# Attention units of the paired blocks: q and k loaded eight tokens to a partition, scores as two 32-row products, and the second weights' preparation on a new timetable

## The chip, the cores and the metric

One core of one Trainium2 chip. The metric is the device time of one execution in microseconds (us). The kernel before takes 1783.91 us, the median of 3 runs (1781.94 to 1783.98).

## The reference

Three layers in a row over 4608 tokens (8 sequences of 576) of 512 features. All inputs are float32.

```python
scores = scale * np.matmul(q_c, k_c.transpose(0, 1, 2, 4, 3))   # chunks of 64 tokens, 8 heads of 64
attn = np.exp(scores - np.max(scores, axis=-1, keepdims=True))
attn = attn / (np.sum(attn, axis=-1, keepdims=True) + 1e-09)
x = np.matmul(attn, v_c)                                        # back to 4608 x 512
xn = x / rms * rms_g
g = xn @ w_gate                                                 # 512 -> 1536
x = (g * (1.0 / (1.0 + np.exp(-g))) * (xn @ w_val)) @ w_out     # 1536 -> 512
h = x @ w_in                                                    # 512 -> 2048
out = (h * np.clip(h + 3.0, 0.0, 6.0) / 6.0) @ w_out2           # 2048 -> 512
```

## The kernel before, in words

The tokens go in nine blocks of 512. Each float32 operand of a large product is split into a high and a low half, and a product is three matmuls of 128x128 by 512 columns. The program has four stages, each a loop over TensorE's products: blocks 0 to 2 of the first layer one by one; blocks 3 to 8 of it in three **pairs** (two blocks at once, in a scheme of seven products for eight; `product`, L831, for the way up, `mm_down_a`, L845 to L848, for the way down); block 0 of the second layer; and its other blocks in four pairs.

Between the products a clock of **ticks** runs (`tick`, L980). `agenda` holds what is to be written into the program at each tick; entries of a tick are sorted by `turn`. During the first two pairs a tick is two products of six matmuls or one step of the way down, and a pair takes 66 ticks (`PAIR`). The first pair begins at tick `P0` = 72. So the order on every engine is fixed when the program is built, and each engine works its list strictly from the front.

**Attention** for the later blocks is done in units of 256 tokens (`Pair`): load q, k and v; turn q and k with VectorE's 32x32 transposes (`turn_q` L639, `turn_k` L643); scores on TensorE (L655), each a 64x64 product over the 64 features of a head; maximum, subtraction, exponential, sum, share; transpose of the result (L697); product with v (L715). Units 10 to 17 run under the first two pairs, four to a pair; `STEPS_P` says at which tick of a unit each step stands. In `parts_qk` q and k are loaded so that a partition holds 32 features of one token: runs of 128 bytes, 16 DMAs for q and 16 for k of a unit, 24 or 32 of each where a unit crosses the end of a sequence. `some(5)` in `tick` issues up to five of the queued parts at a tick, all from SP. SP also issues the operands of the pairs (`wo`, L409; `wd`, L415), 512 KB each, which `loads.ahead` asks for when a tile has been used up.

**Second weights.** `Stash` prepares the second layer's weights while the pairs run: eight slices, each with four raw loads issued by ScalarE (`sraw`, L234), steps on ScalarE, VectorE and GpSimd (`within`, `merge`, `part`, `half`), and stores back to DRAM, issued by ScalarE too (`keep_in`, L283; `keep_out`, L287). `Stash.plan` has the ticks of the steps from a slice's start; the starts were 6, 33, 58, 86, 112, 134, 153 and 172 ticks after `P0`.

All DMAs of SP and ScalarE take eight completion semaphores in turn, and an issue waits until the DMA that had its semaphore before has landed, whatever its data. `wo`, `wd`, raw weights and many others share one pool of 36 buffers (`wp`).

Of the kernel before, what the change touches and what calls it, by code (L numbers as in the profile page):

```python
# [10 lines left out]
F32 = mybir.dt.float32  # L11
# [3 lines left out]
ALU = mybir.AluOpType  # L15
AX = mybir.AxisListType


def _f32_of(word):
# [23 lines left out]
STEPS_P = (  # L43
    (0, ("turn_q",)),
    (1, ("turn_k",)),
    (3, ("scores", "top")),
    (4, ("less",)),
    (5, ("expo",)),
    (7, ("total", "share")),
    (10, ("trans_p", "out_p")),  # L50
    (12, ("values", "out_x", "square")),
    (13, ("squares",)),
)
STEPS = (
    (0, ("turn_q", "turn_k")),
# [10 lines left out]
def fused_kernel(  # L66
# [13 lines left out]
    nc = tc.nc  # L80
    B, H, S, D = q.shape
    NT, DM = out.shape
    CH = 64
    FA = w_gate.shape[1] // 128
    FB = w_in2.shape[1] // 128
# [4 lines left out]
    NP = H // 2  # L90
    scale = 1.0 / float(D) ** 0.5

    NQ = FB // 2
# [10 lines left out]
    sm_p = ctx.enter_context(tc.tile_pool(name="sm", bufs=4))  # L104
# [9 lines left out]
    PS = ps_p.tile([128, 8, 512], F32, name="PS")  # L114
    yd = [dr_p.tile([128, KD, N], F32, name=f"yd{b}") for b in range(NB)]
    ATT, GB, VB, YB = 0, 2, 3, 4
# [105 lines left out]
    def at(t, fn, *args, turn=2):  # L222
        agenda[t].append((turn, lambda: fn(*args)))
# [43 lines left out]
    class Stash:  # L267
# [40 lines left out]
        def plan(self, t0):  # L308
            self.h = {}
            r, w = self.r, self.w  # L310
            for d, fn, *args in (
                (0, r[0].load), (1, r[1].load), (3, r[0].within), (4, r[0].merge), (5, r[0].part),
                (6, self.keep_in, 0), (6, r[1].within), (7, r[1].merge), (8, r[1].part),
                (10, self.keep_in, 1), (10, self.sums), (11, self.half, 0), (11, w[0].load),
                (13, self.keep_in, 2), (13, self.half, 1), (14, w[1].load),
                (15, self.keep_in, 3), (16, w[0].within), (17, w[0].merge), (18, w[0].part),
                (19, self.keep_out, 0), (19, w[1].within), (20, w[1].merge), (21, w[1].part),
                (23, self.keep_out, 1),
            ):
                at(t0 + d, fn, *args, turn=4)  # L320

        def fetch_out(self, z):
            w = wp.tile([128, 2, 512], F32R, tag="w", name="w")
# [22 lines left out]
    stash = [Stash(i) for i in range(NQ)]  # L346
# [76 lines left out]
    def runs(t0, n):  # L423
        done = 0
        while done < n:
            b, s = divmod(t0 + done, S)
            step = min(n - done, S - s)
            yield done, step, b, s
            done += step

    class Att:
# [54 lines left out]
        def top(self):  # L486
            self.mx = sm_p.tile([128, 2, NP], F32, tag="mx", name="mx")
            nc.vector.tensor_reduce(out=self.mx, in_=self.s, axis=AX.X, op=ALU.max)
# [96 lines left out]
        def run(self, *steps):  # L585
            for st in steps:
                getattr(self, st)()
# [4 lines left out]
    class Pair:  # L592
# [13 lines left out]
        def parts_qk(self):  # L606

            self.q, self.k = self.buf("q"), self.buf("k")
            for dst, src in ((self.q, q), (self.k, k)):
                d = dst.rearrange("p (a u f) -> p a u f", a=NP, f=32)  # L610
                for off, n, b, s in runs(self.i * TP, TP):
                    u0, un = off // 32, n // 32
                    sv = src[b, :, s:s + n, :].rearrange("(a j) (u t) (g f) -> j g t a u f", j=2, t=32, f=32)
                    for j in range(2):
                        for g in range(2):
                            r = j * 64 + g * 32
                            if un < NP:
                                for u in range(un):
                                    nc.sync.dma_start(out=d[r:r + 32, :, u0 + u, :], in_=sv[j, g, :, :, u])
                                    yield  # L620
                            else:
                                for a in range(NP):
                                    nc.sync.dma_start(out=d[r:r + 32, a, u0:u0 + un, :], in_=sv[j, g, :, a])  # L623
                                    yield

        def parts_v(self):
            self.v = self.buf("v")
            d = self.v.rearrange("p (c a d) -> p c a d", a=NP, d=D)
            for off, n, b, s in runs(self.i * TP, TP):
                c = slice(off // CH, (off + n) // CH)  # L630
                for r in range(2):
                    for a in range(NP):
                        sv = v[b, 2 * a + (r ^ a & 1), s:s + n, :].rearrange("(c p) d -> p c d", p=CH)
                        nc.sync.dma_start(out=d[r * 64:(r + 1) * 64, c, a, :], in_=sv)
                        yield

        def turn_q(self):
            self.qT = self.buf("qT")
            nc.vector.transpose(out=self.qT, in_=self.q)  # L639

        def turn_k(self):
            self.kT = self.buf("kT")
            nc.vector.transpose(out=self.kT, in_=self.k)  # L643

        def scores(self):
            ps = PS[:, ATT:ATT + 2, :].rearrange("p j (t a k) -> p j t a k", t=2, a=NP)
# [95 lines left out]
                op=ALU.add,  # L742
            )

        def run(self, *steps):
            for st in steps:
                getattr(self, st)()

    XN = {}

# [120 lines left out]
    def split_act(t):  # L871
        hi = ah_p.tile([128, N], F32R, tag="ah", name="ah")
        lo = al_p.tile([128, N], F32R, tag="al", name="al")
        nc.scalar.copy(hi, t)  # L874
        nc.gpsimd.tensor_tensor(lo, t, hi.bitcast(F32), op=ALU.subtract)  # L875
        return hi, lo
# [32 lines left out]
    with tc.manual_schedule():  # L909
# [18 lines left out]
        sqs.pop(0)  # L928
        xf.pop(0)

        unit = [Pair(i) for i in range(NPR)]
        supply = deque()
        ready = set()

        def some(n):

            while n > 0 and supply:
                if next(supply[0][1], True):
                    ready.add(supply.popleft()[0])
                else:  # L940
                    n -= 1
# [38 lines left out]
        def tick():  # L980
            t = clock[0]
            for _, fn in sorted(agenda.pop(t, ()), key=lambda x: x[0]):
                fn()
            some(8 if t < 0 else 5)
            clock[0] += 1

        for blk, due in (
            (1, (-5, -4, -4, -4, -4, -4)), (2, (18, 19, 20, 21, 22, 23)), (3, (42, 43, 44, 45, 46, 47)),
            (4, (66, 67, 67, 67, 67, 67)),
            *((5 + n, tuple(P0 + n // 2 * PAIR + t for t in ((27, 29, 30, 31, 32, 33), (55, 57, 58, 58, 59, 60))[n % 2]))  # L990
              for n in range(4)),
        ):
            Rms(blk).plan(due)
        for i, t0 in (
            (2, -29), (3, -17), (4, -5), (5, 7), (6, 19), (7, 31), (8, 43), (9, 55),
            *((10 + 4 * p + n, P0 + p * PAIR + t) for p in range(2) for n, t in enumerate((0, 14, 29, 42))),
        ):
            plan_unit(i, t0)
        for n in range(2 * NI):
            Operands(*divmod(n, 2)).plan(5 * n + (n > 6) - 2 * (n == 6))  # L1000
        for f in range(FA):
            at(2 * f + 1, keep_w, f, turn=3)
        for i, t0 in enumerate((6, 33, 58, 86, 112, 134, 153, 172)):
            stash[i].plan(P0 + t0)

        S00, S01, S11, S3, S1, S2, S4 = range(7)
# [70 lines left out]
        fills = {p: x_ops(3 + 2 * p) for p in range(3)}  # L1077
        for p, t0 in ((0, 60), (1, P0 + PAIR - 14), (2, P0 + 2 * PAIR - 14)):
            for t in range(t0, t0 + 20):
                at(t, go, fills[p], 2 if p == 0 and t > 71 or p and t in (t0 + 9, t0 + 10) else 1)  # L1080
            for t in range(6):
                at((66 if p == 0 else P0 + p * PAIR - 8) + t, loads.ahead, 1)

# [46 lines left out]
        for p in range(3):  # L1130
# [91 lines left out]
            for n, (z, f) in enumerate(items):  # L1222
                if 0 < n < len(items) - 2:
                    nx.append(split_wp(gt(items[n + 2][1], items[n + 2][0])))
                mm_down_a(loads.t[p, "out", f, 0], nx[n], f == 0, f == FA - 1, yb[z])
                if f == FA - 1:
                    y_store(b + z, yb[z])
                if z == 0 and n < 6:
                    loads.ahead(1)
                if p == 2:  # L1230
                    if n == 12:
                        load_x2(0)
                        XS = [xn_p.tile([128, KD, N], F32R, tag=tag, name="xr") for tag in ("XH", "XL")]
                        xs[:] = [(XS[0][:, c, :], XS[1][:, c, :]) for c in range(KD)]
                    elif n == 18:
                        x2 = xf.pop(0)
                        x_split([x2[:, c, :] for c in range(KD)])
                        stream.ahead(6)
                    z = n - 2 if n < FB else n - 8
                    if n < FB and 0 <= z or n >= FB and FB - 2 <= z < FB:  # L1240
                        stash[z // 2].fetch_out(z % 2)
                tick()

        X = {}
# [52 lines left out]
        for f in range(FB):  # L1297
            bank = 6 + f % 2
            i, z = divmod(f, 2)
            low, top = ((0, 0), (2, 0)) if z == 0 else ((3, 0), (3, 1))  # L1300
            w2 = (stream.t[i, low[0]][:, low[1]], stream.t[i, top[0]][:, top[1]])
            mm_up(bank, lambda wi, c: w2[c // 2][:, wi, c % 2 * 128:(c % 2 + 1) * 128], xs)
            if z == 1:
                stream.ahead(3)
            s = sg_p.tile([128, N], F32, tag="sg", name="sg")
            relu(s, PS[:, bank, :])
            gate(s, PS[:, bank, :])
            a = split_act(s)
            if f > 0:
                go(fill, 2)  # L1310
            if prev is not None:
                mm_down_b(W["out2", f - 1], prev, f == 1, False, base=2)
            prev = a
# [96 lines left out]
```

## Time and profile before

| | |
|---|---|
| median of 3 runs | 1783.91 us |
| the profiled execution | 1777.24 us |
| its span, first to last instruction | 1775.5 us |
| TensorE busy (matmul) | 1687.8 us, 95% |
| VectorE, ScalarE, GpSimd busy | 55%, 41%, 31% |
| HBM | 180 GB/s over the span |

The profile's page has busy times by engine, 40 slices of the span, DMA queues, the chain of work that ended last, and groups of instructions. Other views of the same trace list one engine in order of time, who waited for whom, one source line with the minimum, median and maximum of its durations, and busy times of chosen stretches. PE is TensorE, PEld its weight loads, DVE VectorE, ACT ScalarE, POOL GpSimd, SP SyncE; a q behind a name (SPq, ACTq) is the engine's own sequencer, where DMAs are issued.

### The profile page before, as it was taken

What the parts mean: (1) busy time and instruction counts of PE and PEld (TensorE: products, weight loads), DVE (VectorE), ACT (ScalarE), POOL (GpSimd) and SP (SyncE); (2) the same over time, 40 slices, a digit from 0 to 9 for tenths busy, and PEclk for the clock granted to TensorE, in tenths of its full rate; (3) what the DMA queues carried; (4) which work ended last, traced back from release to release, by engine and by line L of the source; (5) the groups of instructions that cost most, each with busy time, mean ns of one, the idle gap of its engine ahead of it and who ended that gap; (6) DMA issues with size and microseconds to landing.
All of it is one profiled execution on the core that took longest, in us unless ns stands there. A gap on an engine that the chain in (4) does not pass through costs nothing.

```text
span 1775.5 us, 25261 instructions
## 1 busy us (share of the span) xinstructions
PE 1687.8 (95%) x9448; PEld 1376.1 (78%) x9448; DVE 985.3 (55%) x1372; ACT 724.0 (41%) x1119; POOL 551.9 (31%) x408
## 2 busy tenths in 40 slices
PE   4789999999898898899999999999999999999998
PEld 4567777887676676778888888888888888888887
DVE  7997655747454574567654433544554554465440
ACT  5454443544453444454544333333333333343332
POOL 2322434321224522255234622112411321141123
PEclk7799999999998999999999999999999999999999
DMA  9832776656786767885798864444144424423410
GB/s 261 238 71 35 215 229 184 171 146 191 212 266 197 212 204 210 269 279 188 268 323 288 336 230 166 173 142 162 60 157 140 142 97 141 142 95 142 143 67 29
DMA packets 321499, 320.49 MB, mean 181 GB/s; under 512 B 200416, under 2 KB 258784, under 8 KB 321248
## 3 DMA queue, kind: packets, MB, share of 16 engines
q1 hardware_dynamic: 264032, 248.60, 45.4%
q10 hardware_dynamic: 57344, 70.27, 11.4%
q8 instruction: 75, 1.23, 0.3%
q14 instruction: 48, 0.39, 0.1%
HBM read 246.42 MB, written 72.35 MB: 180 GB/s over the span
## 4 chain that ended last, share of the span: by engine, by line
PE 73%; DMA 9%; DVE 8%; SPq 4%; ACT 2%; issue 2%; POOL 1%; ACTq 0%; DVEq 0%; POOLq 0%
PE PS L831 30%; PE PS L820 8%; PE PS L853 7%; PE PS L854 7%; PE PS L857 7%; DMA wo<-ops 3%; PE PS L845 3%; PE PS L848 3%; PE PS L846 3%; SPq L623 2%; DVE w L194 1%; DMA v<-in_v_dram 1%; DMA wraw<-in_moe_w_out_dram 1%; PE PS L715 1%; DMA k<-in_k_dram 1%
## 5 line engine op out<-in xcount | busy, mean ns | idle before, releaser
L831 PE MATMUL PS<-xu,wo 128*128 128x512 f32 x1512 | 356.9, 395 | 20.0 <-DMA wo<-ops 13.9
L831 PEld LDWEIGHTS PS<-xu,wo 128*128 128x128 f32 x1512 | 284.0, 190 | 86.0 <-DMA wo<-ops 9.4
L831 PE MATMUL PS<-xo,wq 128*128 128x512 f32 x1344 | 309.2, 389 | 0.0
L875 POOL TENSOR_TENSOR al<-sg,ah 128x512 fp32r<-128x512 f32 x84 | 120.5, 1434 | 582.4 <-PE PS L857 294.2
L831 PEld LDWEIGHTS PS<-xo,wq 128*128 128x128 f32 x1344 | 252.2, 188 | 52.4
L853 PE MATMUL PS<-w,ah 128*128 128x512 f32 x576 | 224.2, 389 | 0.0
L854 PE MATMUL PS<-w,ah 128*128 128x512 f32 x576 | 224.1, 389 | 0.0
L820 PE MATMUL PS<-XH,w 128*128 128x512 f32 x576 | 150.5, 403 | 11.3 <-DVE sg L1104 5.5
L857 PE MATMUL PS<-w,al 128*128 128x512 f32 x576 | 154.3, 389 | 0.0
L820 PEld LDWEIGHTS PS<-XH,w 128*128 128x128 f32 x576 | 109.5, 193 | 39.6 <-DVE sg L1104 6.9
L853 PEld LDWEIGHTS PS<-w,ah 128*128 128x128 f32 x576 | 108.1, 188 | 22.7 <-ACT ah L874 0.3
L854 PEld LDWEIGHTS PS<-w,ah 128*128 128x128 f32 x576 | 108.2, 188 | 22.5
L857 PEld LDWEIGHTS PS<-w,al 128*128 128x128 f32 x576 | 108.1, 188 | 22.4
L845 PE MATMUL PS<-gs,wd 128*128 128x512 f32 x288 | 115.5, 401 | 9.2 <-ACT gs L1123 4.2
L846 PE MATMUL PS<-gs,wd 128*128 128x512 f32 x288 | 113.4, 394 | 0.0
L1333 DVE TENSOR_TENSOR u<-u,PS 128x512 f32<-128x512 f32 x32 | 22.0, 688 | 156.4 <-PE PS L831 147.3
L1124 POOL TENSOR_TENSOR gs<-gu,gs 128x512 fp32r<-128x512 f32 x60 | 84.3, 1420 | 46.8 <-ACT gs L1123 41.5
L874 ACT CAST ah<-sg 128x512 fp32r<-128x512 f32 x84 | 52.2, 621 | 98.6 <-DVE sg L1104 69.8
L1128 DVE TENSOR_TENSOR gu<-gu,PS 128x512 f32<-128x512 f32 x60 | 40.9, 683 | 72.7 <-PE PS L831 34.3
L242 DVE TENSOR_SCALAR sc<-sc 128x512 f32<-128x512 f32 x32 | 19.7, 616 | 108.6 <-ACT sc L241 89.1
L820 PE MATMUL PS<-XL,w 128*128 128x512 f32 x288 | 79.2, 397 | 0.0
L848 PE MATMUL PS<-gs,wd 128*128 128x512 f32 x288 | 78.5, 395 | 0.1
(198 smaller groups left out, 2693.6 us busy)
## 6 DMA issues: line engine op xcount, KB each, us to landing
wq<-stash_in SPq DMA_DIRECT2D x152, 512.0 KB, 3.9
wo<-ops SPq DMA_DIRECT2D x126, 512.0 KB, 5.7
wd<-keep_out SPq DMA_DIRECT2D x36, 512.0 KB, 5.2
ops<-w ACTq DMA_DIRECT2D x36, 256.0 KB, 3.5
yd<-yst SPq DMA_DIRECT2D x18, 512.0 KB, 4.0
sraw<-in_moe_w_in_dram ACTq DMA_DIRECT2D x16, 512.0 KB, 6.8
stash_in<-slo ACTq DMA_DIRECT2D x32, 256.0 KB, 4.5
sraw<-in_moe_w_out_dram ACTq DMA_DIRECT2D x16, 512.0 KB, 5.3
```

What stands on the lines that cost most here:

```text
L820: nc.tensor.matmul(ps, w(wi, c), xs[c][xi], start=(i == 0), stop=(i == n - 1))
L831: nc.tensor.matmul(PS[:, bank, :], op[:, wi, c * 128:(c + 1) * 128], x[xi][:, c, :], start=first and i == 0, stop=last and i == 5, skip_gr ...
L845: nc.tensor.matmul(ps, wm[0], a[0], start=first, stop=False)
L846: nc.tensor.matmul(ps, wm[1], a[0], start=False, stop=False)
L848: nc.tensor.matmul(PS[:, banks[m], :], w[:, 0, m * 128:(m + 1) * 128], a[1], start=False, stop=last)
L853: nc.tensor.matmul(PS[:, base + m, :], am, w[:, 0, :], start=first, stop=False)
L854: nc.tensor.matmul(PS[:, base + m, :], am, w[:, 1, :], start=False, stop=False)
L857: nc.tensor.matmul(PS[:, base + m, :], a[1][:, m * 128:(m + 1) * 128], w[:, 0, :], start=False, stop=last)
L874: nc.scalar.copy(hi, t)
L875: nc.gpsimd.tensor_tensor(lo, t, hi.bitcast(F32), op=ALU.subtract)
L1124: nc.gpsimd.tensor_tensor(w[:, 1, :], t, w[:, 0, :].bitcast(F32), op=ALU.subtract)
L1128: nc.vector.tensor_tensor(o, x, y, op=op)
```

## The change

Units 10 to 17 become `Wide`, a subclass of `Pair`. A partition now holds eight tokens of one head in a run of 2 KB; four DMAs load q and four k (eight and eight across a sequence's end). The transposes write with a step of eight elements, so that the tokens come out in order, and a head's 64 features come to lie in two pieces on the same 32 partitions. So each score is two products over 32 rows that add up in PSUM, and the scores go in two halves (`scores0`, `scores1`), two ticks apart, each with a maximum of its own. The steps of a unit stand up to one tick later. `some` issues three parts at a tick instead of five from 14 ticks before `P0` on. The slices of the second weights start every 24 ticks and their steps are further apart; stores are written first in their tick instead of last; the last slice ends with the first tick of block 0 of the second layer, where a tick has been added to each step, and its two stored tiles are fetched at step 4 there.

```diff
 STEPS_P = (
     (0, ("turn_q",)),
     (1, ("turn_k",)),
-    (3, ("scores", "top")),
-    (4, ("less",)),
-    (5, ("expo",)),
-    (7, ("total", "share")),
-    (10, ("trans_p", "out_p")),
-    (12, ("values", "out_x", "square")),
-    (13, ("squares",)),
+    (3, ("scores0", "top0")),
+    (5, ("scores1", "top1")),
+    (6, ("less",)),
+    (7, ("expo",)),
+    (9, ("total", "share")),
+    (11, ("trans_p", "out_p")),
+    (13, ("values", "out_x", "square")),
+    (14, ("squares",)),
 )
...
                 (0, r[0].load), (1, r[1].load), (3, r[0].within), (4, r[0].merge), (5, r[0].part),
-                (6, self.keep_in, 0), (6, r[1].within), (7, r[1].merge), (8, r[1].part),
-                (10, self.keep_in, 1), (10, self.sums), (11, self.half, 0), (11, w[0].load),
-                (13, self.keep_in, 2), (13, self.half, 1), (14, w[1].load),
-                (15, self.keep_in, 3), (16, w[0].within), (17, w[0].merge), (18, w[0].part),
-                (19, self.keep_out, 0), (19, w[1].within), (20, w[1].merge), (21, w[1].part),
-                (23, self.keep_out, 1),
+                (9, r[1].within), (10, r[1].merge), (11, r[1].part), (13, self.sums),
+                (14, self.half, 0), (14, w[0].load), (18, self.half, 1), (18, w[1].load),
+                (19, w[0].within), (20, w[0].merge), (21, w[0].part),
+                (25, w[1].within), (26, w[1].merge), (27, w[1].part),
             ):
                 at(t0 + d, fn, *args, turn=4)
+            for d, fn, n in (
+                (7, self.keep_in, 0), (13, self.keep_in, 1), (16, self.keep_in, 2), (20, self.keep_in, 3),
+                (23, self.keep_out, 0), (29, self.keep_out, 1),
+            ):
+                at(t0 + d, fn, n, turn=1)
...
+    class Wide(Pair):
+        def parts_qk(self):
+            self.q, self.k = self.buf("q"), self.buf("k")
+            for dst, src in ((self.q, q), (self.k, k)):
+                d = dst.rearrange("p (h x) -> p h x", h=2)
+                for off, n, b, s in runs(self.i * TP, TP):
+                    for g in range(4):
+                        h = g // 2 + 2 * (g % 2)
+                        sv = src[b, h:h + 5:4, s:s + n, :].rearrange("h (t u) d -> t h (u d)", u=8)
+                        r = g * 32 + off // 8
+                        nc.sync.dma_start(out=d[r:r + n // 8], in_=sv)
+                        yield
+        def turned(self, to, x):
+            nc.vector.transpose(
+                out=to.rearrange("p (h g t u) -> p h u g t", h=2, g=2, u=8),
+                in_=x.rearrange("p (h u g f) -> p h u g f", h=2, u=8, g=2),
+            )
+        def scores(self, e):
...
+            for t in range(2):
+                for h in range(2):
+                    for g in range(2):
+                        for c in range(2):
+                            for j in range(2):
+                                f = slice((2 * j + e) * 32, (2 * j + e + 1) * 32)
+                                n = slice((2 * t + c) * 64, (2 * t + c + 1) * 64)
+                                nc.tensor.matmul(
+                                    ps[c * 64:(c + 1) * 64, j, t, 2 * h + e, :],
+                                    qT[f, g, h, n],
+                                    kT[f, g, h, n],
+                                    start=g == 0,
+                                    stop=g == 1,
+                                )
...
-        unit = [Pair(i) for i in range(NPR)]
+        unit = [(Pair if i < 10 else Wide)(i) for i in range(NPR)]
...
-            some(8 if t < 0 else 5)
+            some(8 if t < 0 else 5 if t < P0 - 14 else 3)
...
-            *((10 + 4 * p + n, P0 + p * PAIR + t) for p in range(2) for n, t in enumerate((0, 14, 29, 42))),
+            *((10 + 4 * p + n, P0 + p * PAIR + t) for p in range(2) for n, t in enumerate((0, 14, 28, 42))),
...
-        for i, t0 in enumerate((6, 33, 58, 86, 112, 134, 153, 172)):
+        for i, t0 in enumerate(range(1, 1 + 24 * NQ, 24)):
             stash[i].plan(P0 + t0)
```

On **SP**, at the start of the first pair: the order before, from the last operand tile asked for ahead of it. `q<-in_q_dram` and `k<-in_k_dram` are parts of unit 11, `wo<-ops_133` and so on the pairs' operands; x5 is five in a row.

```order
L409 DMA wo<-ops_133 128x1024 x2
L619 DMA q<-in_q_dram 32x4x32 x5
L409 DMA wo<-ops_134 128x1024
L619 DMA q<-in_q_dram 32x4x32 x3
L623 DMA q<-in_q_dram 32x6x32 x2
L409 DMA wo<-ops_134 128x1024
L623 DMA q<-in_q_dram 32x6x32 x5
L409 DMA wo<-ops_134 128x1024
L623 DMA q<-in_q_dram 32x6x32 x5
L409 DMA wo<-ops_134 128x1024
```

The same place in the changed program:

```order
L413 DMA wo<-ops_133 128x1024 x2
L772 DMA q<-in_q_dram 8x2x512 x3
L413 DMA wo<-ops_134 128x1024
L772 DMA q<-in_q_dram 8x2x512
L772 DMA q<-in_q_dram 24x2x512 x2
L413 DMA wo<-ops_134 128x1024
L772 DMA q<-in_q_dram 24x2x512 x2
L772 DMA k<-in_k_dram 8x2x512
L413 DMA wo<-ops_134 128x1024
```

Between the same operand loads stand at most three parts instead of five; q of this unit is through after 8 parts instead of 24, and the whole list has 80 parts of q and k for units 11 to 17 instead of 288.

On **PE**, unit 10 in the first pair before (`kT,qT` are scores, `ident,p` the transposes of the result, `qT,v` the products with v, `xu,wo` the pair's products):

```order
L831 MATMUL PS<-xu,wo 128x512 x48
L655 MATMUL PS<-kT,qT 64x64 x32
L831 MATMUL PS<-xu,wo 128x512 x84
L697 MATMUL PS<-ident,p 128x128 x8
L831 MATMUL PS<-xu,wo 128x512 x24
L715 MATMUL PS<-qT,v 64x64 x32
```

and in the changed program:

```order
L891 MATMUL PS<-xu,wo 128x512 x48
L794 MATMUL PS<-kT,qT 64x64 x32
L891 MATMUL PS<-xu,wo 128x512 x24
L794 MATMUL PS<-kT,qT 64x64 x32
L891 MATMUL PS<-xu,wo 128x512 x72
L704 MATMUL PS<-ident,p 128x128 x8
L891 MATMUL PS<-xu,wo 128x512 x24
L722 MATMUL PS<-qT,v 64x64 x32
```

A unit now breaks into the large products four times instead of three, with 32 more small products.

## Rows read from the trace of the kernel before

**Rows 1.** Busy times by stretch: first, second, third pair; second layer. (us, then by engine)

```profile
412.60:637.50 224.90, 206.35 (x1341) 164.74 (x1341) 128.18 (x161) 102.20 (x156) 74.92 (x53) 0.96 0.74 217
637.50:849.40 211.90, 199.43 (x1341) 160.67 (x1340) 127.63 (x162) 103.72 (x158) 77.96 (x55) 0.99 0.74 230
849.40:1030.60 181.20, 180.19 (x793) 148.53 (x793) 87.21 (x117) 76.26 (x132) 79.61 (x58) 1.00 0.86 311
1030.60:1775.50 744.90, 740.18 (x3265) 612.35 (x3263) 347.68 (x484) 246.72 (x388) 190.85 (x144) 1.00 0.37 130
```

**Rows 2.** Chain that ended last, second layer: start, us, what.

```profile
1142.46 9.52 PE PS L831 x42
```

**Rows 3.** PE in order of time, unit 10: start, us, what.

```profile
423.62 1.16 PE L655 MATMUL PS<-kT,qT 64*64 64x64 f32 x64
424.72 19.34 PE L831 MATMUL PS<-xu,wo 128*128 128x512 f32 x84
443.90 1.03 PE L697 MATMUL PS<-ident,p 128*128 128x128 f32 x8
444.69 5.70 PE L831 MATMUL PS<-xu,wo 128*128 128x512 f32 x24
450.32 1.16 PE L715 MATMUL PS<-qT,v 64*64 64x64 f32 x64
451.41 0.97 PE L831 MATMUL PS<-xu,wo 128*128 128x512 f32 x3
```

**Rows 4.** PE's waits, first two pairs: us in total, times, longest us.

```profile
PE PS L831 <- DMA wo<-ops: 13.9, 8, 3.9
PE PS L845 <- ACT gs L1123: 4.2, 3, 2.2
PE PS L845 <- DVE gu L1128: 2.8, 2, 2.2
...
PE PS L655 <- DVE kT L643: 2.7, 1, 2.7
```

**Rows 5.** SP in order of time, first pair: start, us, what.

```profile
474.82 1.22 SPq L409 DMA_DIRECT2D wo<-ops  x2
476.09 6.44 SPq L623 DMA_DIRECT2D q<-in_q_dram  x10
482.57 0.99 SPq L409 DMA_DIRECT2D wo<-ops  x2
```

**Rows 6.** SP's waits, first two pairs: us in total, times, longest us.

```profile
SPq L623 <- DMA wo<-ops: 25.7, 23, 2.7
...
SPq L634 <- DMA wo<-ops: 8.8, 8, 2.4
SPq L409 <- DMA stash_in<-shi: 7.2, 1, 7.2
```

**Rows 7.** Lines L623 and L634: ns of one issue, minimum, median, maximum.

```profile
L623 SPq DMA_DIRECT2D q<-in_q_dram x128: 311/439/1224, 423.0 to 760.2; - x128
...
L634 SPq DMA_DIRECT2D v<-in_v_dram x80: 465/606/1232, 455.8 to 789.3; - x80
```

**Rows 8.** ACT's waits, first two pairs: us in total, times, longest us.

```profile
ACT gu L1199 <- DMA k<-in_k_dram: 8.6, 2, 6.3
ACT sc L241 <- DMA k<-in_k_dram: 8.3, 4, 4.1
```

**Rows 9.** DMA issues, first two pairs: count, KB each, us to landing.

```profile
stash_in<-slo ACTq DMA_DIRECT2D x20, 256.0 KB, 3.8
...
q<-in_q_dram SPq DMA_DIRECT2D x64, 32.0 KB, 3.6
```

**Rows 10.** Lines L655, L643 and L738: ns of one, minimum, median, maximum.

```profile
L655 PEld LDWEIGHTS PS<-kT,qT x1024: 129/135/223, 91.0 to 792.0; 64*64 64x64 f32 x171
...
L643 DVE STREAM_TRANSPOSE kT<-k x16: 1186/1203/1246, 89.1 to 784.9; 128x1024 f32<-128x1024 f32 x16
...
L738 DVE TENSOR_REDUCE sqs<-kT x16: 1958/1986/2054, 125.5 to 821.0; 128x256 f32<-128x1024 f32 x16
```

More of the change, by code (lines that the diff above doesn't have):

```diff
@@ L635, in parts_v @@
                         yield
+        def turned(self, to, x):
+            nc.vector.transpose(out=to, in_=x)
         def turn_q(self):
             self.qT = self.buf("qT")
-            nc.vector.transpose(out=self.qT, in_=self.q)
+            self.turned(self.qT, self.q)
         def turn_k(self):
             self.kT = self.buf("kT")
-            nc.vector.transpose(out=self.kT, in_=self.k)
+            self.turned(self.kT, self.k)
         def scores(self):
@@ L743, in squares, with run, turned, top @@
             )
-        def run(self, *steps):
-            for st in steps:
+        def run(self, st):
+            if st[-1].isdigit():
+                getattr(self, st[:-1])(int(st[-1]))
+            else:
                 getattr(self, st)()
+    class Wide(Pair):
[10 more added lines that the diff above has]
+                        yield
+        def turned(self, to, x):
+            nc.vector.transpose(
[3 more added lines that the diff above has]
+        def scores(self, e):
+            ps = PS[:, ATT:ATT + 2, :].rearrange("p j (t a k) -> p j t a k", t=2, a=NP)
+            self.s = PS[:, ATT:ATT + 2, :].rearrange("p j (x k) -> p j x k", k=CH)
+            qT, kT = (
+                x.rearrange("p (h g n) -> p g h n", h=2, g=2) for x in (self.qT, self.kT)
+            )
[12 more added lines that the diff above has]
+                                    stop=g == 1,
+                                )
+        def top(self, e):
+            if e == 0:
+                self.mx = sm_p.tile([128, 2, 2 * NP], F32, tag="mx", name="mx")
+            nc.vector.tensor_reduce(
+                out=self.mx[:, :, e::2], in_=self.s[:, :, e::2, :], axis=AX.X, op=ALU.max
+            )
@@ L989, in fused_kernel @@
             (4, (66, 67, 67, 67, 67, 67)),
-            *((5 + n, tuple(P0 + n // 2 * PAIR + t for t in ((27, 29, 30, 31, 32, 33), (55, 57, 58, 58, 59, 60))[n % 2]))
+            *((5 + n, tuple(P0 + n // 2 * PAIR + t for t in ((28, 30, 31, 32, 33, 34), (56, 58, 59, 59, 60, 61))[n % 2]))
               for n in range(4)),
@@ L1079, in fused_kernel @@
             for t in range(t0, t0 + 20):
-                at(t, go, fills[p], 2 if p == 0 and t > 71 or p and t in (t0 + 9, t0 + 10) else 1)
+                at(t, go, fills[p], 2 if p == 0 and t > 71 or p and t in (t0 + 10, t0 + 11) else 1)
             for t in range(6):
@@ L1238, in fused_kernel @@
                         stream.ahead(6)
-                    z = n - 2 if n < FB else n - 8
-                    if n < FB and 0 <= z or n >= FB and FB - 2 <= z < FB:
-                        stash[z // 2].fetch_out(z % 2)
+                    if 1 < n < FB:
+                        stash[(n - 2) // 2].fetch_out(n % 2)
                 tick()
@@ L1308, in fused_kernel @@
             a = split_act(s)
+            tick()
+            if f == 4:
+                for z in range(2):
+                    stash[NQ - 1].fetch_out(z)
             if f > 0:
```

## The prediction

> **What bounds the kernel now.** I first cut the span into stages. In the second layer TensorE is busy for 740.18 of 744.9 us at the full 2.4 GHz clock (granted 1.00), and nothing there can be gained except with fewer products [rows 1]. The chain that ended last gives the price of a product: 42 in 9.52 us, 0.2267 us each [rows 2]. A pair has 7 x 6 x 12 = 504 products on its way up and 24 x 12 = 288 on its way down, 792 in all, so 792 x 0.2267 = 179.5 us. The third pair, which has no attention in it, takes 181.2 us: it is at that price. The first takes 224.9 and the second 211.9 us [rows 1], so 45.4 and 32.4 us more than their products.
>
> Part of that is attention on TensorE. From the start of unit 10's scores (423.62) to the product after its last step (451.41) pass 27.79 us, in which 84 + 24 products stand: 24.48 us [rows 3]. So a unit costs 3.31 us, four of them 13.2, and the two sums for the root mean square of a pair about 0.9 us (four products). The first pair then loses 45.4 - 14.1 = 31.3 us and the second 18.3 us, **49.6 us together**, to something that the third does not have. This is all that the change can win back.
>
> What is it? PE's longest waits in the two pairs are for operand tiles, 13.9 us; then come waits for ScalarE's and VectorE's results, 4.2 and 2.8 us, and 2.7 us for a turned k [rows 4]. The granted clock is 0.96 and 0.99 there [rows 1]: after an idle stretch the array goes at 1.2 GHz for a while. A mean of 0.96 over 224.9 us is 8% of the time at half speed, some 9 us lost beside the idle time; 0.99 is some 2 us.
>
> Why are the tiles late? SP's order of time shows it: two operand tiles issued at 474.82, then ten parts of q, 6.44 us, and only then the next two tiles at 482.57 [rows 5]. So two tiles go out in 7.75 us, while TensorE uses one up in two products of six matmuls, 2.7 us. One issue of q takes 0.439 us in the middle (L623, 128 for q, as many for k, and 16 each at L619), one of v 0.606 us [rows 7]. In the two pairs 288 parts of q and k take 288 x 0.439 = 126 us of SP's 437 us. And the parts wait as well: for operand tiles that they have nothing to do with, 25.7 us in 23 waits, and v's parts 8.8 us [rows 6], because DMAs share eight semaphores. The same reaches ScalarE, whose own DMA issues wait for k's parts: its work at L1199 is held 8.6 us by k's loads and at L241 8.3 us [rows 8]. ScalarE's list stands still then, and with it the results that PE waits for. So several of PE's rows have one cause, **too many small DMAs**.
>
> **The change part by part.**
>
> *Loads.* 288 parts become 80. Their issue is not in the trace; the bounds are the shortest q issue, 0.311 us, and v's longest, 1.232 us [rows 7]: 25 to 99 us, against 126. I take 0.44, the nearest form (same queue, same three-dimensional source), so 35 us: SP gets some 91 us back, over 40 us in either pair. A part now carries 128 KB instead of 32; q's landed in 3.6 us, ScalarE's 256 KB stores in 3.8 [rows 9], so I expect under 4 us, and a semaphore is held no longer than now. With at most three parts to a tick instead of five, the operand tiles that TensorE needs go out every 2.7 us. Of the 49.6 us I take 40 as won back: the waits for tiles and k and for what ScalarE could not start, and the slow clock behind each. Bounds: 24, if about half only changes its name, and all 49.6.
>
> *Scores.* Eight units have a second half, with as many matmul instructions again, and one more break into the large products. One half is 1.10 us (423.62 to 424.72) [rows 3], and about 0.2 us go at the two edges, since 3.31 is 0.3 more than its three pieces: 1.3 us, x 8 = **10.4 us, on the path**, since TensorE has nothing to hide it under. The lower bound is nothing, if it falls into waits that remain. The upper bound is in rival 3.
>
> *Transposes, maxima.* The transposes now write every eighth element. One takes 1.20 us now; the sum over squares (L738) handles 1024 elements too, but reads them with a long step, and takes 1.99 us [rows 10]. So 16 transposes cost 0 to 0.8 us more each, 13 us at most. VectorE is busy 128.18 of 224.9 us [rows 1] and PE's waits for it are 2.8 us [rows 4], so I take nothing; if the cover is gone, rival 2. The Trainium skill (SBUF — State Buffer, section "Door 1: The DMA port swizzle") says that accesses which leave a 16-byte line at each element pay a penalty, and eight float32 are 32 bytes. By that rule the transposes are slower; L738's row agrees with it, and the sum would be up to 13 us worse. The maximum in two halves costs VectorE an instruction more per unit, under the same cover.
>
> *Second weights.* The same steps on the same engines, 24 ticks apart instead of 19 to 28, with more room between steps, so a store waits less for the engine that makes its data, and ScalarE behind it too. The first two pairs get slightly more of it, and the end of the last slice falls into block 0 of the second layer, which has no slack; one store and two fetched tiles there have ten steps of time. I take zero, from 2 us less to 4 more.
>
> **Sum.** -40 + 10.4 = -29.6 us, so -30. The profiled execution took 1777.24 us, of which 1775.5 are the span, and would become 1747; it lies 6.7 us under the median, which I take as the base: 1783.9 - 30 = **1754 us**.
>
> **Rivals.**
>
> 1. *New waits take over half.* ScalarE, VectorE and GpSimd carry slightly more of the second weights in the two pairs, and scores in halves move subtraction and exponential a tick or two closer to the next unit. For it: PE already waits 4.2 and 2.8 us for their results [rows 4]. Against: much of that is held by DMAs [rows 8]. Then 24.8 us come back: 1783.9 - 24.8 + 10.4 = 1769.5. Chance 0.15.
>
> 2. *The step of eight shows.* The transposes cost 13 us more and stand before evictions that PE waits for: 1767. Chance 0.05. That is the rule of the Trainium skill named above, on the path.
>
> 3. *Slower: the 32-row products lose their overlap.* Now a half is 16 rounds of four products on four parts of the array, 0.07 us to a round, and a weight load of 0.135 us hides under them [rows 3, 10]. If with 32 rows it did not hide, each of 16 halves would be 16 x 0.135 = 2.2 us longer: 35 us, and 1754 + 35 = 1789. It decides when a half costs 30 / 16 = 1.9 us more than now. Against it: loads hide now although two neighbours in the order use the same rows, and the new order alternates rows. Chance 0.05.
>
> 4. *The tiles stay late for another reason.* An operand tile's issue also waits for its buffer, 7.2 us once behind a store of the second weights [rows 6]. If only 10 us come back, the scores eat them: 1784. For: the tiles share one pool with the raw weights. Against: such waits are few, the ones behind parts many. Chance 0.05.
>
> **How the numbers follow.** My forecast has 0.70, with 1743 (all 49.6 back, scores 8.8, and a little from ScalarE) to 1764. The range should leave out 2 in 10 at most: 1743 to 1772 adds rivals 1 and 2 and leaves out 3 and 4 and the edges. A measurement tells about 0.2%, 3.6 us, from no change. Faster by more: forecast, rivals 1 and 2, 0.90; within it, mostly rival 4, 0.04; slower, mostly rival 3, 0.06.
>
> **What would show it.** First and second pair take 195 to 210 us each instead of 225 and 212, the third still 181. SP has 80 parts of q and k of about 0.44 us, PE's wait for operand tiles falls from 13.9 us to under 4, the granted clock in the first pair rises to 0.99 or more, ScalarE's waits for k's loads are gone. Each half of the scores takes about 1.1 us. Transposes of 2.0 us speak for rival 2, halves of 3 us for rival 3. I am wrong if the waits for tiles stay, or if their place is taken by waits for ScalarE and VectorE of over 20 us.

## The result, and the profile after

The changed kernel takes 1753.64 us (median of 4 runs, 1748.98 to 1754.57) beside 1783.54 us for the kernel before (median of 4 runs as well): a ratio of 0.9829, with a 95% interval of 0.9810 to 0.9848. The forecast was 1754.

The span of the profiled execution goes from 1775.5 to 1746.8 us. Busy times by stretch, cut at the same places as [rows 1] (us, then PE, PEld, DVE, ACT, POOL busy with their counts, granted clock, DMA share, GB/s):

```profile
411.70:615.30 203.60, 200.65 (x1598) 163.90 (x1597) 133.89 (x167) 101.17 (x156) 76.19 (x54) 1.00 0.79 243
615.30:819.80 204.50, 202.27 (x1597) 163.35 (x1596) 140.71 (x170) 105.89 (x162) 81.82 (x57) 1.00 0.75 247
819.80:1001.20 181.40, 179.78 (x793) 148.59 (x792) 86.54 (x111) 74.32 (x129) 76.92 (x55) 1.00 0.80 290
1001.20:1746.80 745.60, 740.38 (x3265) 612.56 (x3264) 348.09 (x484) 246.93 (x388) 191.08 (x144) 1.00 0.38 131
```

All of it lies in the first two pairs: 224.9 and 211.9 us became 203.6 and 204.5, 28.7 us in all. The third pair and the second layer stayed within 1 us. The clock is granted in full, where it was 0.96 and 0.99. VectorE is busy for 274.6 us there, the two pairs together, instead of 255.8.

Who PE waited for, in the two pairs (us in total, times, longest us), to be held against [rows 4]:

```profile
PE PS L891 <- DVE gu L1188: 2.2, 1, 2.2
PE PS L908 <- POOL gs L1184: 0.8, 1, 0.8
PE PS L794 <- DVE kT L776: 0.7, 2, 0.6
PE PS L905 <- ACT gs L1183: 0.5, 2, 0.3
```

The row of 13.9 us for operand tiles is gone altogether. These are all waits above 0.4 us.

SP in order of time at the beginning of the first pair (start, us, what):

```profile
428.30 0.35 SPq L413 DMA_DIRECT2D wo<-ops  x1
428.70 1.00 SPq L772 DMA_DIRECT2D k<-in_k_dram  x3
430.54 0.35 SPq L413 DMA_DIRECT2D wo<-ops  x1
431.31 3.10 SPq L772 DMA_DIRECT2D k<-in_k_dram  x4
434.57 7.62 SPq L413 DMA_DIRECT2D wo<-ops  x7
```

In [rows 5] it was ten parts of q between two pairs of tiles. After the seven tiles at 434.57 SP comes to the first part of v, for which it waits 11.7 us until TensorE has done its products with v (L722); the part goes out at 454.63. So SP is ahead and waits for TensorE instead of the other way round. Before and after, in the two pairs (us in total, times, longest us):

```profile
SPq L634 <- PE PS L715: 9.3, 4, 3.0
```

```profile
SPq L638 <- PE PS L722: 49.2, 7, 11.7
```

One issue of q or k now takes (L772; ns minimum, median, maximum):

```profile
L772 SPq DMA_DIRECT2D q<-in_q_dram x44: 273/380/1517, 360.4 to 714.5; - x44
L772 SPq DMA_DIRECT2D k<-in_k_dram x44: 273/316/1122, 363.8 to 720.3; - x44
```

Of the 88, eight belong to unit 10 and go out before the first pair. What has not gone away is the waiting of these parts for other DMAs: SP's waits still have

```profile
SPq L772 <- DMA wo<-ops: 29.6, 14, 4.6
```

against 25.7 us in [rows 6]. TensorE no longer waits for a tile behind them. ScalarE's waits for DMAs come to 22 us in the two pairs, where they came to 83. The largest row is 6.4 us, in two pieces:

```profile
ACT gs L1183 <- DMA v<-in_v_dram: 6.4, 2, 4.8
```

and the two rows for k's loads of [rows 8] have no successor.

The scores of unit 10 on PE (start, us, what), and the lines of the scores and of the transposes (ns minimum, median, maximum), beside [rows 3, 10]:

```profile
422.69 1.16 PE L794 MATMUL PS<-kT,qT 32*64 32x64 f32 x64
423.78 5.73 PE L891 MATMUL PS<-xu,wo 128*128 128x512 f32 x24
429.44 1.16 PE L794 MATMUL PS<-kT,qT 32*64 32x64 f32 x64
430.53 16.62 PE L891 MATMUL PS<-xu,wo 128*128 128x512 f32 x72
```

```profile
L794 PEld LDWEIGHTS PS<-kT,qT x1024: 127/133/133, 422.7 to 765.5; 32*64 32x64 f32 x171
...
L776 DVE STREAM_TRANSPOSE qT<-q x8: 2124/2168/2237, 412.7 to 751.9; 128x1024 f32<-128x1024 f32 x8
L776 DVE STREAM_TRANSPOSE kT<-k x8: 2106/2155/2196, 417.1 to 753.9; 128x1024 f32<-128x1024 f32 x8
```

From 423.78 to 430.53 are 6.75 us, of which 24 products take 5.44: a half of the scores costs 1.31 us, at unit 10. The transposes became 0.93 (q) and 0.95 us (k) longer each, and TensorE waited 0.7 us in all for them.

### The profile page after: what moved, and what is told of

It reads as the page before. It is cut to its first block, busy times and chain, and to the rows that moved or that the text cites. A ratio compares the mean times of both kernels' runs of the same rounds, so it can differ in the third digit from the quotient of the medians.

```text
span 1746.8 us, 26052 instructions
## 1 busy us (share of the span) xinstructions
PE 1688.1 (97%) x9960; PEld 1380.9 (79%) x9960; DVE 1002.8 (57%) x1380; ACT 723.2 (41%) x1119; POOL 555.1 (32%) x408
## 4 chain that ended last, share of the span: by engine, by line
PE 52%; DVE 1%; DMA 0%; ACT 0%; issue 0%; POOL 0%; SPq 0%; DVEq 0%; POOLq 0%
PE PS L891 24%; PE PS L913 7%; PE PS L917 7%; PE PS L914 7%; PE PS L880 2%; PE PS L908 1%; PE PS L905 1%; PE PS L906 1%; DMA x<-yd 0%; DVE xf L841 0%; DVE xt L1093 0%; DVE sraw L252 0%; DVE sg L1351 0%; DVE sc L243 0%; POOL al L935 0%
## 5 line engine op out<-in xcount | busy, mean ns | idle before, releaser
L891 PE MATMUL PS<-xu,wo 128*128 128x512 f32 x1512 | 351.9, 392 | 3.0 <-DVE gu L1188 2.2
L905 PE MATMUL PS<-gs,wd 128*128 128x512 f32 x288 | 113.6, 394 | 2.1 <-DVE gu L1188 1.6
L906 PE MATMUL PS<-gs,wd 128*128 128x512 f32 x288 | 112.2, 390 | 0.0
L908 PE MATMUL PS<-gs,wd 128*128 128x512 f32 x288 | 77.1, 390 | 0.8 <-POOL gs L1184 0.8
L950 DVE TENSOR_SCALAR ost<-PS 128x512 f32<-128x512 f32 x26 | 16.5, 685 | 102.1 <-PE PS L917 102.1
```

What stands on the lines that cost most here:

```text
L891: nc.tensor.matmul(PS[:, bank, :], op[:, wi, c * 128:(c + 1) * 128], x[xi][:, c, :], start=first and i == 0, stop=last and i == 5, skip_gr ...
L905: nc.tensor.matmul(ps, wm[0], a[0], start=first, stop=False)
L906: nc.tensor.matmul(ps, wm[1], a[0], start=False, stop=False)
L908: nc.tensor.matmul(PS[:, banks[m], :], w[:, 0, m * 128:(m + 1) * 128], a[1], start=False, stop=last)
```

## The experiments

The kernels ran in three series, each on one chip beside runs of the kernel before. Ratios are to the kernel before, with their 95% intervals. "The pairs" are the first two together, from the profiled execution: 436.8 us before, 408.1 in the changed kernel. A profiled execution is one of several and can lie some 5 to 8 us off the median (1783.92 us for the 224 parts below, with a median of 1778.37), so the pairs' times are no finer than that.

### The new loads and scores without the new timetable

The second weights' starts, steps and the place of the last fetches are those of the kernel before; all else is the change.

```diff
...
-        for i, t0 in enumerate(range(1, 1 + 24 * NQ, 24)):
+        for i, t0 in enumerate((6, 33, 58, 86, 112, 134, 153, 172)):
             stash[i].plan(P0 + t0)
```

> The changed kernel with the second weights on their old starts and steps (and the last slice's fetches where they were). Theory: few DMAs are the whole gain, the timetable about nothing: 1750 to 1760 us, PE waits for operand tiles under 3 us in the first two pairs. Rival: the spread timetable carries a good part, because stores no longer hold ScalarE: 1765 us or more, with waits for ScalarE's and VectorE's results of over 10 us.

Measured: 1750.28 us, 0.9796 (0.9781 to 0.9811); the pairs 406.3 us; no wait of PE for operand tiles. The loads with their pace carry the whole gain, and the timetable none.

### The new timetable alone

The kernel before with the steps, starts, added ticks and fetches of the change's second weights.

```diff
...
-        for i, t0 in enumerate((6, 33, 58, 86, 112, 134, 153, 172)):
+        for i, t0 in enumerate(range(1, 1 + 24 * NQ, 24)):
             stash[i].plan(P0 + t0)
```

> The kernel before with the second weights on the new timetable alone. Theory: within 4 us of the kernel before (1780 to 1788), with the waits for operand tiles still over 10 us. Rival: a part of the gain comes from here: 1775 us or less.

Measured: 1793.57 us, 1.0039 (1.0024 to 1.0054): slower, which neither theory had. The pairs take 451.0 us, 14 more; by the medians it is 8 us. PE's waits there (us in total, times, longest us):

```profile
PE PS L834 <- DMA wo<-ops: 15.3, 9, 3.7
PE PS L658 <- DVE kT L646: 5.8, 1, 5.8
PE PS L834 <- ACT gu L1202: 3.7, 2, 2.9
PE PS L834 <- DVE gu L1131: 3.4, 2, 2.9
```

The operand tiles are as late as before [rows 4]; the waits for VectorE's results have grown from 6.7 to 15.2 us, those for ScalarE's from 9.9 to 10.9. So with the old loads the new timetable does harm. Which of its steps does it was not tried.

### The same runs of 2 KB in many DMAs

Each DMA of the change is cut into pieces of 8 partitions, and five parts go out at a tick as before. That makes 224 parts for units 11 to 17.

```diff
-                        nc.sync.dma_start(out=d[r:r + n // 8], in_=sv)
-                        yield
+                        for y in range(0, n // 8, 8):
+                            nc.sync.dma_start(out=d[r + y:r + y + 8], in_=sv[y:y + 8])
+                            yield
...
-            some(8 if t < 0 else 5 if t < P0 - 14 else 3)
+            some(8 if t < 0 else 5)
```

> The changed kernel with the same 2 KB runs, but each DMA cut into pieces of 8 partitions (224 parts of q and k for units 11 to 17 instead of 80, against 288 before) and five parts a tick again. Theory, the number of DMAs on SP and its eight semaphores: most of the gain goes, the scores' price stays: 1775 to 1795 us, waits for operand tiles of 8 us or more. Rival, the size of the packets and the time that they take on the DMA engines: the gain stays: 1752 to 1758 us.

Measured: 1778.37 us, 0.9967 (0.9949 to 0.9985); the pairs 439.4 us. With runs as long as the change's, about 25 of its 30 us are lost. The waits are not where I had put them, though: PE waits 2.6 us for operand tiles and 3.8 us once for what the trace puts down to one of k's loads, and the rest is spread over ScalarE and VectorE; the clock is 0.98 in both pairs.

```profile
PE PS L892 <- DMA k<-in_k_dram: 3.8, 1, 3.8
...
PE PS L892 <- DMA wo<-ops: 2.6, 2, 2.0
PE PS L892 <- DVE s L1189: 2.3, 2, 1.2
PE PS L892 <- DVE gu L1189: 2.3, 1, 2.3
PE PS L892 <- ACT gu L1260: 2.2, 1, 2.2
```

This kernel differs from the change in two things, number and pace, so a second series takes them apart.

### Transposes with a step of eight in the kernel before

```diff
-            nc.vector.transpose(out=self.qT, in_=self.q)
...
+                nc.vector.transpose(
+                    out=self.qT.rearrange("p (h g t u) -> p h u g t", h=2, g=2, u=8),
+                    in_=self.q.rearrange("p (h u g f) -> p h u g f", h=2, u=8, g=2),
+                )
...
```

`k` is turned in the same way, in units 10 to 17 only, and the scores are left as they were.

> The kernel before, whose transposes of units 10 to 17 write with a step of eight elements, so that their result is another arrangement than the scores need; all else as before. Theory: about 2.16 us each instead of 1.2, hidden on VectorE: within 4 us of the kernel before. Rival: VectorE's lists hold TensorE: 5 to 15 us slower.

Measured: 1785.14 us, 1.0004 (0.9989 to 1.0019). The transposes do take longer:

```profile
L652 DVE STREAM_TRANSPOSE kT<-k x8: 2021/2130/2161, 421.0 to 792.5; 128x1024 f32<-128x1024 f32 x8
```

and the time does not move. Their cost, about 15 us of VectorE's time in all, is covered.

### The change once more, beside three of its variants

> The changed kernel once more, beside the next three on one chip: 0.981 to 0.985 of the kernel before.

Measured: 1753.7 us, 0.9821 (0.9801 to 0.9842).

> The changed kernel with the second weights on the old timetable, once more: theory, the new timetable is worth nothing, so within 0.2% of the changed kernel; rival, it costs some 3 us, as the first run of it suggests (0.9796 against 0.9829), and this is a version faster than both.

Measured: 1749.75 us, 0.9798 (0.9778 to 0.9819). Two series agree that the old timetable is some 4 us better (0.9796 and 0.9798 against 0.9829 and 0.9821); the intervals still overlap by a little, so this is likely and not shown.

### Five parts to a tick in the change

```diff
-            some(8 if t < 0 else 5 if t < P0 - 14 else 3)
+            some(8 if t < 0 else 5)
```

> The changed kernel with five parts to a tick instead of three. Theory: with 80 parts in all it makes no difference, within 4 us of the changed kernel, and the loss of the run with 224 parts is due to their number. Rival: parts in bunches of five hold the operand tiles up, 5 to 10 us slower than the changed kernel.

Measured: 1768.92 us, 0.9914 (0.9895 to 0.9933): 15 us slower than the change beside it; the pairs 421.7 us, where that one's take 411.8. My theory fell here: with 80 parts of q and k, too, it matters how densely they stand. The pace holds for all queued parts, so for v's 80 parts in the two pairs as well; whether it matters for q and k or for v was not separated. SP at the same place of the first pair, in order of time (start, us, what):

```profile
424.23 0.36 SPq L413 DMA_DIRECT2D wo<-ops  x1
426.55 6.15 SPq L772 DMA_DIRECT2D q<-in_q_dram  x3
432.80 0.61 SPq L772 DMA_DIRECT2D k<-in_k_dram  x2
433.51 0.35 SPq L413 DMA_DIRECT2D wo<-ops  x1
```

Three parts of q take 6.15 us, but 5.1 us of that is one wait, for a raw weight tile of ScalarE's (SP's waits from 424 to 434):

```profile
SPq L772 <- DMA sraw<-in_moe_w_in_dram: 5.1, 1, 5.1
```

Two operand tiles are 9.3 us apart. Yet TensorE waits only 1.0 us for operand tiles in the two pairs (0.8 in the change beside it), so the rival's reason is not borne out either; its waits for VectorE's results are 9.6 us, where the change beside it has 3.6. Later in the second pair the tiles then go out in a bunch, and ScalarE stands still for a raw weight tile that it had asked for at 656.87, in the middle of it:

```profile
654.18 7.81 SPq L413 DMA_DIRECT2D wo<-ops  x8
```

```profile
656.87 0.66 ACTq L235 DMA_DIRECT2D sraw<-in_moe_w_in_dram  x1
...
668.15 0.66 ACT L242 ACTIVATE sc<-sraw 128x512 f32<-128x512 f32 x1 [3.94 <-DMA sraw<-in_moe_w_in_dram]
```

At 667.15 TensorE stops for 3.3 us, the longest stop in the two pairs of this run. That the bunch causes the stop is argued from these rows and was not tried by itself. A bunch alone is not enough: the change issues seven tiles in a row at 434.57, and TensorE does not stop there. So what makes the denser pace cost 15 us stays open.

### Half of the scores' products

```diff
-                    for g in range(2):
+                    for g in range(1):
...
-                                    stop=g == 1,
+                                    stop=True,
```

> The changed kernel without the second of the two 32-row products of each score, so half of each score's sum is left out. Theory: the products are on the path, a half takes 0.55 us instead of 1.1, 16 halves: 8 to 9 us faster than the changed kernel. Rival: they fall into waits that are there anyway: within 3 us of it.

Measured: 1749.3 us, 0.9797 (0.9777 to 0.9818): 4.4 us faster than the change beside it, between the two. TensorE's waits grew at the same time (for VectorE's `s` from 0.2 to 1.8 us, for ScalarE's `gu` from 1.0 to 1.7), so part of what is saved is waited for.

### Pace without number, number without pace

The kernel before at four parts to a tick, and the 224 parts of 2 KB runs at four parts to a tick. The edit shown is the first kernel's; the second has the split of the run with 224 parts, and four for the change's three.

```diff
-            some(8 if t < 0 else 5)
+            some(8 if t < 0 else 5 if t < P0 - 14 else 4)
```

> The kernel before with four parts to a tick instead of five in the pairs. Theory, the number of parts: the same 368 parts have to go out, those that do not fit go in a bunch ahead of the transposes, within 5 us of the kernel before. Rival, the pace alone is worth what it was worth in the changed kernel (15 us between three and five): 8 us or more faster.

Measured: 1784.87 us, 1.0003 (0.9992 to 1.0014). Four parts to a tick are worth nothing in the kernel before. But the pace cannot be set by itself there: unit 13 has 64 parts of q and k, and from the turning of unit 12's k to its own start are 12 ticks, which take 48 at four a tick. The other 16 go out in a bunch just ahead of the transposes (SP, start, us, what), and TensorE waits for the turned k once, for 8.2 us, beside 17.1 us for operand tiles:

```profile
562.54 7.49 SPq L623 DMA_DIRECT2D k<-in_k_dram  x16
```

```profile
PE PS L831 <- DMA wo<-ops: 17.1, 9, 3.7
PE PS L655 <- DVE kT L643: 8.2, 1, 8.2
```

> The changed kernel with its 2 KB runs cut into 224 parts as before in this series, at four parts to a tick instead of five. Theory, the number of DMAs: still 10 us or more behind the same kernel with 80 parts (1753.7), so 1764 to 1780. Rival, only the pace counts: 1753 to 1761.

Measured: 1770.53 us, 0.9923 (0.9903 to 0.9943): 17 us behind the 80 parts at three. Together, the 2 KB kernels are in order: 224 parts at five to a tick 0.9967, 224 at four 0.9923, 80 at five 0.9914, 80 at three 0.9821. Both number and pace count: at five to a tick 224 parts are slower than 80, and at either number the denser pace is slower, each time with intervals that do not overlap. The 17 us are both together; 80 parts at four and 224 at three were not run.

### A slower pace on the old timetable

```diff
-            some(8 if t < 0 else 5 if t < P0 - 14 else 3)
+            some(8 if t < 0 else 5 if t < P0 - 14 else 2)
```

on top of the new loads with the old timetable.

> The changed loads and scores with the old timetable of the second weights and two parts to a tick. Theory: a slower pace leaves operand tiles still better off, 1744 to 1750 us. Rival: parts come too late for their unit and the transposes wait, 1752 us or more.

Measured: 1746.16 us, 0.9782 (0.9768 to 0.9797), the fastest complete kernel here, and faster than the change. What two parts to a tick gain over three on the old timetable (0.9796 and 0.9798) is within the noise. Its first two pairs:

```profile
415.00:616.20 201.20, 200.89 (x1597) 164.19 (x1596) 129.60 (x162) 101.62 (x154) 75.03 (x53) 1.00 0.79 242
616.20:817.10 200.90, 200.49 (x1597) 163.90 (x1596) 132.31 (x166) 104.21 (x158) 77.69 (x55) 1.00 0.76 243
```

The only wait of PE that is left there is 0.6 us for VectorE. A pair's products, its attention and the second halves come to 179.5 + 14.1 + 5.2 = 198.8 us, so 4.5 us are left to be had in the two pairs.

### Half of the scores' products on the old timetable

Two edits from above together, at three parts to a tick: the old timetable, and the second products left out.

> The changed loads with the old timetable, without the second 32-row product of each score (half of each score's sum left out). Theory: the scores' products are on the path where no other wait is left, 7 to 9 us faster than 1750, so 1741 to 1743. Rival, as with the new timetable: 4 us or less, 1746 or more.

Measured: 1742.81 us, 0.9761 (0.9747 to 0.9776): 7 us faster than the same kernel with all products in the other two series (1749.75 and 1750.28). Here a half goes from 424.46 to 425.08, 0.62 us where it was 1.09:

```profile
424.46 0.69 PE L791 MATMUL PS<-kT,qT 32*64 32x64 f32 x32
425.08 5.73 PE L888 MATMUL PS<-xu,wo 128*128 128x512 f32 x24
```

16 x 0.47 = 7.5 us; nearly all of it shows. So where nothing else holds TensorE up, the scores lie on the path at their full price.

## Why the prediction was right

**The loss to be won back.** 49.6 us were put down to waits and their slow clock in the two pairs, of which 40 were to come back. After, each pair's floor is 198.8 us (with 5.2 for its second halves), and 203.6 and 204.5 were needed: 10.5 us are left, so 39.1 came back, if each second half costs what unit 10's does. The clock rose to 1.00, as said.

**The scores.** 1.3 us for each second half, 10.4 us on the path: the trace has 1.31 us. The kernel without the second products on the old timetable shows that such products are paid for in full on TensorE; on the new one nearly half of the saving is lost to other waits (4.4 us of 7.5 show). The weight loads still hide (0.133 us each, and a half takes as long as the whole did), so rival 3, the slower end, did not come about.

**The loads.** Bounds of 0.311 to 1.232 us for an issue, 0.44 taken: 0.38 and 0.32 in the middle. The sum "91 us of SP's time back" was right in kind, but the step behind it, that the number of parts alone decides, was too simple. The runs with five parts to a tick show that the same 80 parts, set more densely, give half of the gain back, and the run with 224 parts at four to a tick that the number counts as well. The prediction named the three parts to a tick in one sentence and gave it no size; it is worth 15 us here, for parts of q, k and v together. The kernel before could not have used it: units 11, 13 and 15 have 48 or 64 parts of q and k, which do not go into the 12 or 13 ticks before them at three. So that the forecast of 40 us was met is in part luck: by the count of parts alone, five to a tick would have had to win back as much, and that kernel took 1768.92 us.

**The transposes.** I gave them 0 to 0.8 us more each; they took 0.93 and 0.95 more, beyond the bound from the sum over squares. The Trainium skill's rule on accesses that leave a 16-byte line (SBUF — State Buffer, "Door 1: The DMA port swizzle") spoke for the slower side, and the trace agrees with it here: 2.16 us against 1.20 (k) and 1.24 (q, median of L639). That all of it is covered, as the sum had it, is shown by the kernel before with the same transposes, at 1.0004, and in the change by the 0.7 us that TensorE waits for them. So rival 2 fell on the path, not on the price.

**The second weights.** Zero, from 2 us less to 4 more, was the term; some 4 us more is what two pairs of runs suggest. In the kernel before it costs 7 us by the ratio (1.0039). My reason, that stores would hold ScalarE less, did not show in the time; why the new timetable costs is open. Rival 4, tiles late because of their buffers, is answered by the wait for tiles that is gone.

**Open.** The 224 parts at five to a tick beat the kernel before by 6 us (0.9967) although they carry the price of the scores and of the new timetable. Whether that is the fewer parts (224 for 288) or the longer runs was not separated; loads of 128-byte runs in as few DMAs were not tried. Nor was the way found by which a denser pace reaches TensorE: the waits for operand tiles, by which the prediction had explained the loss, are 13.9 us before and only 1.0 us with five to a tick, and ScalarE's waits for DMAs are 25 us there, close to the change's 22.

## What to carry to other kernels

Where one queue issues small loads among the operand tiles that the bounding engine lives from, look at that queue in order of time and count issues per tile used up; here fewer and larger loads paid even though they made VectorE work more, because it had cover. Then set the pace anew: what the smaller number allows can be worth as much as the number. A second edit that travels with the first (here the timetable) is to be timed alone; it may cost something that the first one hides.

## What the runs showed that I had not expected

Writing 32x32 transposes with a step of eight float32 costs VectorE 0.93 to 0.95 us more per 1024 elements a partition, 75 to 79% more than the contiguous form. Products over 32 rows on two row groups and two column groups run at the rate of 64-row ones (64 instructions in 1.09 us, beside 1.10). And issuing the parts of q, k and v (80 of 32 to 128 KB and 80 of 16 to 64 KB) at five to a tick instead of three costs 15 us of 1754, with the same bytes and the same instructions.
